# The order of twelve products in an out projection: four float32r products first, or one page at a time

## The chip, the cores and the metric

The kernel runs on one core of one Trainium2 chip. The metric is the device time of one execution in microseconds (us); the time given is the median of several runs.

## The reference

Attention over pooled keys and values, followed by a gated feed-forward layer (SwiGLU) on the 4608 resulting rows:

```python
k_p = k.reshape(B, H, Sp, pool, D).mean(axis=3)          # B=8, H=8, S=576, D=64, pool=8
v_p = v.reshape(B, H, Sp, pool, D).mean(axis=3)
scores = scale * np.matmul(q, k_p.transpose(0, 1, 3, 2))
attn = softmax(scores)
x = np.matmul(attn, v_p) ...                              # as 4608 rows of 512
g = x @ w_gate                                            # 512 x 1536
silu = g * (1.0 / (1.0 + np.exp(-g)))
val = x @ w_val                                           # 512 x 1536
out = silu * val @ w_out                                  # 1536 x 512
```

## The kernel before

The 4608 rows are cut into nine tiles of 512 (`TILE`). The hidden width of 1536 is cut into twelve chunks of 128 (`NCH`), the output width of 512 into four pages of 128 (`NJ`). Everything is computed transposed: the hidden unit or output column lies on the partition, the 512 rows of a tile on the free axis.

To keep float32 precision, each operand of a product is split into a high and a low part. For a tile and a chunk, `side` issues twelve float16 products for the gate and twelve for the value (lines L797 to L799: high by high, high by low, low by high, for each of four slices of x), each into one PSUM bank (`gv`). From these, ScalarE and VectorE make the hidden value h of the chunk, and three copies of it: `hh` (float32r, L1076), `hb` (bfloat16, L1077) and the rest `hl` (bfloat16, L1080).

The out projection of a chunk, `project`, adds the chunk's part to the four pages of the output, which are four PSUM banks `acc`, one for each page j. Each page takes three products of 512 columns: `wo_h` by `hh` in float32r (L824), the weights in bfloat16 by `hl` (L830) and `wo_l` by `hb` (L831), twelve in all. A float32r matmul loads its weights itself (the trace shows it as a load and a matmul of one line); a bfloat16 product has a load instruction of its own ahead of it.

The first tile is written out by hand, with the loading of weights and the first attention pieces between its steps. From the second tile on, `hidden_tiles` runs the loop: for each tile i and chunk c, gate products, value products, the copies of h, and then `flush()`, which issues the projection of the chunk before (its operands have been ready for long; after the last chunk its own projection follows at once). Behind a tile's last projection `store` copies the four pages to SBUF, by VectorE and ScalarE in turn (L838), and issues a DMA for each (L839).

The attention of later tiles runs in the background. At four points of each chunk `slot(vector, scalar)` is called, which issues whichever pieces of it fit: scores (L542, L543), the subtraction of the maximum (L552, L553), values (L658, L659), sums over partitions (L181, L182), and copies, loads and transposes. One of the four points lies inside the projection: it is handed to `project` as `between`, and called after the four float32r products. In the first tile `project` has no `between`.

The order of instructions on each engine is the order in which the program writes them (a manual schedule).

Of the kernel before, what the change touches and what calls it, by code (L numbers as in the profile page):

```python
# [17 lines left out]
P = 128  # L18
# [67 lines left out]
def attention_then_swiglu(  # L86
# [11 lines left out]
    nc = tc.nc  # L98
    B, _, NJ, S = q.shape
# [49 lines left out]
    wo_h = const.tile([P, NCH, DM], F32R, name="wo_h")  # L149
# [668 lines left out]

    def project(acc, c, a, e, hh, hb, hl, begin, end, between=None, wo=wo_b):
        n = e - a  # L820
        for j in range(NJ):
            o = acc[j][:, a:e]
            js = slice(j * P, (j + 1) * P)
            nc.tensor.matmul(o, wo_h[:, c, js], hh[:, :n], start=begin, stop=False)  # L824
        if between:
            between()
        for j in range(NJ):
            o = acc[j][:, a:e]
            js = slice(j * P, (j + 1) * P)
            nc.tensor.matmul(o, wo[:, c, js], hl[:, :n], start=False, stop=False)  # L830
            nc.tensor.matmul(o, wo_l[:, c, js], hb[:, :n], start=False, stop=end)  # L831

    def store(t, acc):
        lo, n, _ = t
        for p in range(NJ // 2):
            ob = mid.tile([P, 2, TILE], F32, name="ob", tag="mid")[:, :, :n]
            for j, copy in ((2 * p, nc.vector.tensor_copy), (2 * p + 1, nc.scalar.copy)):
                copy(out=ob[:, j % 2], in_=acc[j][:, :n])  # L838
                nc.sync.dma_start(out=out[j * P : (j + 1) * P, lo : lo + n], in_=ob[:, j % 2])  # L839
# [67 lines left out]
    def first_tile():  # L907
# [69 lines left out]
        def step_out(k):  # L977
            t = steps[k]
            hb = t["hh"].bitcast(BF16).rearrange("p (n t) -> p n t", t=2)[:, :, 1]
            end = k == len(steps) - 1  # L980
            project(kept["acc"], *t["at"], t["hh"], hb, t["hl"], False, end, wo=wo_up)
# [58 lines left out]
    def hidden_tiles():  # L1040
# [4 lines left out]
        def flush():  # L1045
            if pending:
                acc, last, i, c, *rest = pending.pop()
                wo = wo_b if i > 2 else wo_up
                project(acc(), c, 0, tiles[i][1], *rest, c == 0, last, lambda: slot(*ROOM[2]), wo)
                if last:  # L1050
                    store(tiles[i], acc())
# [92 lines left out]
```

## Time and profile before

| | |
|---|---|
| median of 3 runs | 977.51 us (976.91 to 977.65) |
| profiled execution | 975.54 us, span 973.8 us |
| TensorE matmuls busy | 939.7 us (97%) |
| VectorE, ScalarE, GpSimd busy | 566.0, 461.2, 241.3 us |
| TensorE clock granted | 0.993 of full speed on average |

In a row of the timeline stand the start in us from the span's start, the duration, the engine (PE is TensorE's matmul, PEld its weight load, DVE VectorE, ACT ScalarE, SPq the queue that issues DMAs), the line, the operation, the tiles that it writes and reads, shapes and count, and in brackets the idle time of the engine before it and what ended that. Successive equal instructions are merged into one row. Matmuls are pipelined: the recorded time of one overlaps the next, so the distance from start to start is what one costs. A row of a stretch gives its length, then busy time and count of PE, PEld, DVE, ACT and POOL, the granted clock, the DMA share and GB/s.

### The profile page before, as it was taken

To read this page: it belongs to the slowest core of one execution; us is meant where nothing else is said; L and a number is where in the kernel's file an instruction comes from. 1 tells how busy PE (TensorE), PEld (TensorE's weight loads), DVE (VectorE), ACT (ScalarE), POOL (GpSimd) and SP (SyncE) were. 2 spreads that over 40 slices of the span, in tenths; PEclk is the share of its full clock that TensorE was granted. 3 is DMA by queue.
4 is the path that set the end of the run, shared out by engine and by line. 5 is a ranking of instruction groups with operands and counts; after the bars stand their busy time and mean duration, and the time that the engine had idled before them with its cause. 6 is when DMAs were issued, how large, how long until landed. Compare 5 with 4: busy or idle time off the path is not lost.

```text
span 973.8 us, 14306 instructions
## 1 busy us (share of the span) xinstructions
PE 939.7 (97%) x5486; PEld 498.4 (51%) x5486; DVE 566.0 (58%) x1005; ACT 461.2 (47%) x864; POOL 241.3 (25%) x327
## 2 busy tenths in 40 slices
PE   5779999799999999999999999999999999999998
PEld 4657545354555555554555555554545555444443
DVE  6788877667766675586446675674444454323222
ACT  3898883245554553544254544552454443222222
POOL 4533336035226230521025211620121201000000
PEclk9899999999999999999999999999999999999999
DMA  9855426246437342653047232840231222001001
GB/s 349 237 154 208 154 109 171 80 115 186 92 109 211 102 83 79 187 127 82 13 88 235 57 70 87 251 86 15 77 83 43 71 66 55 11 1 44 0 1 44
DMA packets 155524, 103.02 MB, mean 106 GB/s; under 512 B 113216, under 2 KB 141888, under 8 KB 153920
## 3 DMA queue, kind: packets, MB, share of 16 engines
q1 hardware_dynamic: 155456, 102.11, 37.3%
q8 instruction: 43, 0.70, 0.3%
q14 instruction: 25, 0.20, 0.1%
HBM read 67.63 MB, written 9.44 MB: 79 GB/s over the span
## 4 chain that ended last, share of the span: by engine, by line
PE 87%; DMA 6%; POOL 2%; ACT 2%; issue 1%; DVE 1%; SPq 0%; POOLq 0%; DVEq 0%; ACTq 0%
PE gv L797 18%; PE gv L798 18%; PE gv L799 18%; PE acc L824 10%; PE acc L830 9%; PE acc L831 9%; DMA pt<-half 2%; DMA kr<-k_rows 1%; DMA in<-v_rest 1%; DMA in<-k_rows 1%; PE ps L542 1%; PE ps L658 1%; PE ps L543 1%; PE ps L659 1%; DMA k<-k_rows 1%
## 5 line engine op out<-in xcount | busy, mean ns | idle before, releaser
L797 PE MATMUL gv<-x,wgv_h 128*128 128x512 f16 (+1 forms) x888 | 332.0, 374 | 3.8 <-ACT x L669 1.8
L798 PE MATMUL gv<-x,wgv_h 128*128 128x512 f16 (+1 forms) x888 | 331.8, 374 | 1.3 <-DVE x L673 1.3
L799 PE MATMUL gv<-x,wgv_l 128*128 128x512 f16 (+1 forms) x888 | 331.9, 374 | 0.5 <-DVE wgv_l L253 0.5
L810 DVE SCALAR_TENSOR_TENSOR hf<-hf,gv 128x512 f32<-128x512 f32 (+1 forms) x111 | 74.1, 668 | 171.6 <-ACT hf L807 171.3
L807 ACT ACTIVATE hf<-gv,un 128x512 f32<-128x512 f32 (+1 forms) x111 | 74.8, 674 | 193.9 <-PE gv L799 193.9
L1076 ACT CAST hh<-gv 128x512 fp32r<-128x512 f32 x96 | 56.3, 586 | 227.2 <-DVE gv L815 227.2
L831 PE MATMUL acc<-hb,wo_l 128*128 128x512 bf16 x384 | 145.5, 379 | 0.0
L824 PE MATMUL acc<-hh,wo_h 128*128 128x512 f32 (+1 forms) x444 | 139.5, 436 | 0.0
L799 PEld LDWEIGHTS <-wgv_l 128*128 128x128 f16 x888 | 87.0, 98 | 102.2 <-issue 1.7
L798 PEld LDWEIGHTS <-wgv_h 128*128 128x128 f16 x888 | 87.0, 98 | 98.1 <-issue 4.7
L797 PEld LDWEIGHTS <-wgv_h 128*128 128x128 f16 x888 | 87.4, 98 | 94.3
L1080 DVE TENSOR_TENSOR hl<-gv,hh 128x512 bf16<-128x512 f32 x96 | 66.3, 691 | 111.0 <-ACT hb L1077 111.0
L525 POOL TENSOR_TENSOR box<-qt,box 64x512 f16<-64x512 f32 (+1 forms) x60 | 64.0, 1067 | 227.8 <-issue 160.9
L815 DVE SCALAR_TENSOR_TENSOR gv<-gv,un,hf 128x512 f32<-128x512 f32 (+1 forms) x111 | 82.3, 741 | 63.0 <-PE gv L799 62.3
L830 PE MATMUL acc<-hl,wo_b 128*128 128x512 bf16 x288 | 109.8, 381 | 0.0
L824 PEld LDWEIGHTS acc<-hh,wo_h 128*128 128x128 f32 x444 | 83.2, 191 | 24.2 <-ACT hh L969 0.3
L630 POOL TENSOR_TENSOR half<-sc,half 128x512 f16<-128x512 f32 (+1 forms) x30 | 34.7, 1158 | 215.8 <-ACT half L620 193.6
L831 PEld LDWEIGHTS <-wo_l 128*128 128x128 bf16 x444 | 43.7, 98 | 37.9
L1077 ACT CAST hb<-gv 128x512 bf16<-128x512 f32 x96 | 56.8, 591 | 0.0
L830 PE MATMUL acc<-hl,wo_h 128*128 128x512 bf16 (+1 forms) x156 | 56.7, 368 | 0.0
L830 PEld LDWEIGHTS <-wo_b 128*128 128x128 bf16 x288 | 28.3, 98 | 42.2 <-issue 16.6
L523 ACT ACTIVATE qt<-qt,inv 128x512 f32<-128x512 f32 (+1 forms) x60 | 40.9, 682 | 0.0
(143 smaller groups left out, 1121.5 us busy)
## 6 DMA issues: line engine op xcount, KB each, us to landing
ws<-w_all SPq DMA_DIRECT2D x12, 1536.0 KB, 7.1
qt<-q_twice SPq DMA_DIRECT2D x48, 256.0 KB, 3.2
out_t<-ob SPq DMA_DIRECT2D x36, 256.0 KB, 2.3
in<-k_rows SPq DMA_DIRECT2D x12, 576.0 KB, 3.9
in<-q_rows SPq DMA_DIRECT2D x12, 576.0 KB, 5.2
in<-v_main SPq DMA_DIRECT2D x12, 512.0 KB, 4.3
in<-v_rest SPq DMA_DIRECT2D x12, 512.0 KB, 5.7
qt<-q_rows SPq DMA_DIRECT2D x8, 256.0 KB, 4.3
```

The lines of the kernel that those rows point to most:

```text
L525: nc.gpsimd.tensor_sub(o[rows], qt[rows], o[rows])
L797: nc.tensor.matmul(o, wh, x["h"][:, j, a:e], start=(j == 0), stop=False)
L798: nc.tensor.matmul(o, wh, x["l"][:, j, a:e], start=False, stop=False)
L799: nc.tensor.matmul(o, wl, x["h"][:, j, a:e], start=False, stop=(j == NJ - 1))
L807: nc.scalar.activation(hf, gate, AF.Tanh, scale=un[:, c, 0:1])
L810: nc.vector.scalar_tensor_tensor(out=hf, in0=hf, scalar=1.0, in1=gate, op0=ALU.add, op1=ALU.mult)
L815: nc.vector.scalar_tensor_tensor(out=out, in0=val, scalar=un[:, c, 2:3], in1=hf, op0=ALU.mult, op1=ALU.mult)
L824: nc.tensor.matmul(o, wo_h[:, c, js], hh[:, :n], start=begin, stop=False)
L830: nc.tensor.matmul(o, wo[:, c, js], hl[:, :n], start=False, stop=False)
L831: nc.tensor.matmul(o, wo_l[:, c, js], hb[:, :n], start=False, stop=end)
L1077: nc.scalar.copy(hb[:, :n], val)
L1080: nc.vector.tensor_sub(hl[:, :n], val, hh[:, :n].bitcast(F32))
```

## The change

Where `project` is given a `between`, that is in the 96 projections of the second to ninth tile, the twelve products are issued page by page: one float32r product, then the two bfloat16 ones of the same page. The slot's background work is called after two pages. Without `between`, in the first tile, the order stays as it was.

```diff
     def project(acc, c, a, e, hh, hb, hl, begin, end, between=None, wo=wo_b):
         n = e - a
-        for j in range(NJ):
-            o = acc[j][:, a:e]
+
+        def high(j):
             js = slice(j * P, (j + 1) * P)
-            nc.tensor.matmul(o, wo_h[:, c, js], hh[:, :n], start=begin, stop=False)
-        if between:
-            between()
-        for j in range(NJ):
-            o = acc[j][:, a:e]
-            js = slice(j * P, (j + 1) * P)
+            nc.tensor.matmul(acc[j][:, a:e], wo_h[:, c, js], hh[:, :n], start=begin, stop=False)
+
+        def low(j):
+            o, js = acc[j][:, a:e], slice(j * P, (j + 1) * P)
             nc.tensor.matmul(o, wo[:, c, js], hl[:, :n], start=False, stop=False)
             nc.tensor.matmul(o, wo_l[:, c, js], hb[:, :n], start=False, stop=end)
+
+        if between:
+            for j in range(NJ):
+                if j == NJ // 2:
+                    between()
+                high(j)
+                low(j)
+            return
+        for j in range(NJ):
+            high(j)
+        for j in range(NJ):
+            low(j)
```

On TensorE, the last projection of the program stood like this before (`acc_8681` to `acc_8684` are the four pages; the rest repeats for the other pages):

```order
L824 MATMUL acc_8681<-hh,wo_h 128x512
L824 MATMUL acc_8682<-hh,wo_h 128x512
L824 MATMUL acc_8683<-hh,wo_h 128x512
L824 MATMUL acc_8684<-hh,wo_h 128x512
L830 LDWEIGHTS wo_b
L830 MATMUL acc_8681<-hl,wo_b 128x512
L831 LDWEIGHTS wo_l
L831 MATMUL acc_8681<-hb,wo_l 128x512
```

and with the change, where the two bfloat16 lines are L828 and L829, its first two pages are:

```order
L824 MATMUL acc_8681<-hh,wo_h 128x512
L828 LDWEIGHTS wo_b
L828 MATMUL acc_8681<-hl,wo_b 128x512
L829 LDWEIGHTS wo_l
L829 MATMUL acc_8681<-hb,wo_l 128x512
L824 MATMUL acc_8682<-hh,wo_h 128x512
L828 LDWEIGHTS wo_b
L828 MATMUL acc_8682<-hl,wo_b 128x512
L829 LDWEIGHTS wo_l
L829 MATMUL acc_8682<-hb,wo_l 128x512
```

Each float32r product now has bfloat16 products on both sides, and each page's last product comes three after that of the page before, where it came two after.

In 20 of the 96 projections the slot inside issues small matmuls. On TensorE, at the end of the values of one such projection (`pt` the attention weights, `box` the values, `acc_5005` to `acc_5008` the pages), before:

```order
L659 LDWEIGHTS pt
L659 MATMUL ps<-box,pt 128x64
L830 LDWEIGHTS wo_b
L830 MATMUL acc_5005<-hl,wo_b 128x512
L831 LDWEIGHTS wo_l
L831 MATMUL acc_5005<-hb,wo_l 128x512
```

and with the change:

```order
L659 LDWEIGHTS pt
L659 MATMUL ps<-box,pt 128x64
L824 MATMUL acc_5007<-hh,wo_h 128x512
L828 LDWEIGHTS wo_b
L828 MATMUL acc_5007<-hl,wo_b 128x512
L829 LDWEIGHTS wo_l
L829 MATMUL acc_5007<-hb,wo_l 128x512
```

The small matmuls are now followed by the float32r product of the third page; ahead of them stand six products of the projection, where four stood. On the other engines and in the DMA queue the order is unchanged.

## The prediction

> **What bounds the kernel now.** I read the page's totals first, then the chain that ended last, then the busy time of a late stretch, and only then single rows on TensorE.
>
> ```profile
> span 973.8 us, 14306 instructions
> PE 939.7 (97%) x5486; PEld 498.4 (51%) x5486; DVE 566.0 (58%) x1005; ACT 461.2 (47%) x864; POOL 241.3 (25%) x327
> PE 87%; DMA 6%; POOL 2%; ACT 2%; issue 1%; DVE 1%; SPq 0%; POOLq 0%; DVEq 0%; ACTq 0%
> ...
> 510.00:810.00 300.00, 300.00 (x1759) 152.70 (x1758) 170.08 (x308) 138.26 (x279) 70.48 (x94) 1.00 0.35 95
> ...
> PE ps L658 <- issue: 1.0, 1, 1.0
> PE ps L658 <- DVE sc L553: 0.5, 1, 0.5
> ```
>
> The fourth line is a stretch of the trace, from 510 to 810 us: TensorE is busy for all of its 300 us, the other engines for less than 60% of it, and the granted clock is 1.00. The last two lines are all waits of TensorE that the list of waits has from 190 us to the end: 1.5 us. So in the part that the change touches (from the second tile on), the time is the sum of the distances between matmul starts, and any nanosecond added to a distance is added to the run. Work taken off another engine would buy nothing.
>
> So I need those distances. A matmul's recorded duration (0.38 us) overlaps the next one; only starts count. Here is one out projection, before, with the loads of its weights (PEld); the rows for the second, third and fourth float32r product come from narrow cuts of the same timeline, where they are not merged.
>
> ```profile
> 606.66 0.38 PE L799 MATMUL gv<-x,wgv_l 128*128 128x512 f16 x1
> 606.66 0.87 PEld L824 LDWEIGHTS acc<-hh,wo_h 128*128 128x128 f32 x4
> 607.11 0.39 PE L824 MATMUL acc<-hh,wo_h 128*128 128x512 f32 x1
> 607.34 0.39 PE L824 MATMUL acc<-hh,wo_h 128*128 128x512 f32 x1
> 607.57 0.40 PE L824 MATMUL acc<-hh,wo_h 128*128 128x512 f32 x1
> 607.80 0.10 PEld L830 LDWEIGHTS <-wo_b 128*128 128x128 bf16 x1 [0.27 <-issue]
> 607.81 0.39 PE L830 MATMUL acc<-hl,wo_b 128*128 128x512 bf16 x1
> 608.03 0.38 PE L831 MATMUL acc<-hb,wo_l 128*128 128x512 bf16 x1
> 608.03 0.10 PEld L830 LDWEIGHTS <-wo_b 128*128 128x128 bf16 x1
> ...
> 955.85 0.38 PE L799 MATMUL gv<-x,wgv_l 128*128 128x512 f16 x1
> 957.23 0.38 PE L831 MATMUL acc<-hb,wo_l 128*128 128x512 bf16 x1
> 963.70 0.38 PE L799 MATMUL gv<-x,wgv_l 128*128 128x512 f16 x1
> ```
>
> From 957.23 to 963.70 stand 30 distances between 16-bit products: 6.47 / 30 = 0.2157 us each. From the last 16-bit product ahead of the float32r ones (L799) to the second bfloat16 product behind them (L831) are 6 distances: 1.37 us in the first case, 1.38 in the second, 1.375 as their mean, where six plain ones take 1.294. So a group of four float32r products costs T = 0.081 us more than its length. Where does it sit? Between one float32r product and the next lie 0.46 / 2 = 0.23 us; with the rounding of the rows between 0.2275 and 0.2325. I take 0.231, so each of the three inner distances is r = 0.0155 too long (0.012 to 0.017 by the rounding), 0.046 together. The other 0.035 lie at entry and exit. The exit is plain in the loads: a bfloat16 load normally starts with the product ahead of it (608.03 beside 608.03), but the first one behind a float32r product starts at 607.80, after 0.27 us without a load, just ahead of its own matmul. It is not loaded early.
>
> **The change part by part.** No product, load, copy or transfer is added or removed, and VectorE, ScalarE, GpSimd and the DMA queue keep their orders instruction by instruction. Only TensorE's order changes, in 96 out projections (8 tiles by 12 chunks).
>
> First, the grouping. Before, a projection has one entry and one exit, after, four. Alone, a float32r product costs entry plus exit, T - 3r = 0.081 - 0.046 = 0.035 us. Four cost 0.140, against T = 0.081 for the group: +0.059 in round numbers, and from 3T - 12r with r = 0.0155, 0.243 - 0.186 = +0.057 us. 96 x 0.057 = **+5.5 us**. With r at its rounding bounds it is 0.101 and 0.041 per projection, 9.7 and 3.9 us. The entry is now from a bfloat16 product and not a float16 one; the very last projection of the run shows this case:
>
> ```profile
> 966.37 0.38 PE L831 MATMUL acc<-hb,wo_l 128*128 128x512 bf16 x1
> 966.40 1.28 PE L824 MATMUL acc<-hh,wo_h 128*128 128x512 f32 x4
> 967.52 0.39 PE L830 MATMUL acc<-hl,wo_b 128*128 128x512 bf16 x1
> 967.75 0.38 PE L831 MATMUL acc<-hb,wo_l 128*128 128x512 bf16 x1
> ```
>
> 966.37 to 967.75 is 1.38 us, the same as from float16. A lone float32r product is nowhere in this trace; that its entry and exit cost what a group's do is the step I lean on.
>
> Second, the background work. In 20 projections the slot in the middle issues small matmuls (15 times the values L658 and L659, 4 times these and sums, once sums alone). Before, a bfloat16 product follows them; after, the third page's float32r one.
>
> ```profile
> 616.62 0.19 PE L659 MATMUL ps<-box,pt 128*128 128x64 f16 x1
> 616.65 0.38 PE L830 MATMUL acc<-hl,wo_b 128*128 128x512 bf16 x1
> ...
> 108.84 0.19 PE L649 MATMUL ps<-pt,vst_f 96*128 96x64 f16 x1
> 108.87 1.18 PE L824 MATMUL acc<-hh,wo_h 128*128 128x512 f32 x4
> 110.12 0.39 PE L831 MATMUL acc<-hh,wo_l 128*128 128x512 bf16 x1
> ```
>
> A bfloat16 product comes 0.03 us after a small one (616.62, 616.65), so nothing is exposed. The nearest case of a float32r product behind a small one is in the first tile: from L649 to the second bfloat16 product are 1.28 us. Behind a 512-column product it was 1.375; the small one should save 0.216 - 0.03 = 0.186 but saves 0.095, so 0.09 us of the float32 load stand open. 20 x 0.09 = **+1.8 us**; at least 0, if other loads are ahead, at most 20 x 0.19 = 3.8, if a whole load (0.87 us for four overlapping ones, so about 0.19 from one to its end) shows. I take the row, which is the same pair of kinds.
>
> Third, the slot's work is reached later: two pages (six products) stand ahead of it and not four products. That is two distances more, 0.43 us. Two projections wait there now, for VectorE to be done with the buffer:
>
> ```profile
> 229.65 1.29 PE L824 MATMUL acc<-hh,wo_h 128*128 128x512 f32 x4
> 231.35 0.46 DVE L553 TENSOR_TENSOR sc<-ps,mx 128x288 f32<-128x288 f32 x1
> 231.91 0.19 PE L658 MATMUL ps<-box,pt 128*128 128x64 f16 x1 [0.98 <-issue]
> ...
> 415.22 1.28 PE L824 MATMUL acc<-hh,wo_h 128*128 128x512 f32 x4
> 417.04 0.19 PE L658 MATMUL ps<-box,pt 128*128 128x64 f16 x1 [0.55 <-DVE sc L553]
> ...
> 615.06 1.28 PE L824 MATMUL acc<-hh,wo_h 128*128 128x512 f32 x4
> 616.18 0.20 PE L658 MATMUL ps<-box,pt 128*128 128x64 f16 x1
> ```
>
> Undisturbed, L658 comes 1.12 us after the group's first record (615.06, 616.18); here 2.26 and 1.82, so 1.14 and 0.70 us are waited. VectorE's time is set by its own queue, so bfloat16 products that now run in the wait take 0.43 us off each: **-0.9 us** (0 if VectorE shifts along, -1.85 if both waits go). The values come 0.43 us later for those behind them, VectorE and ScalarE, which idle 40% and more; I cost that at nothing, and its cover is the rest of the projection and the next 24 products.
>
> Fourth, the end. The pages' last products are now three apart and not two, so copies and stores start earlier, the last one's copy excepted.
>
> ```profile
> 969.46 0.59 ACT L838 COPY ob<-acc 128x512 f32<-128x512 f32 x1 [0.28 <-PE acc L831]
> 969.78 0.40 SPq L839 DMA_DIRECT2D out_t<-ob  x1
> 970.27 0.41 SPq L839 DMA_DIRECT2D out_t<-ob  x1
> ```
>
> The last copy ends at 970.05 but its store is issued at 970.27, behind the third one (to 970.18). With the third one a product (0.22 us) earlier, the last goes out at about 970.1: **-0.2 us**, between 0 and -0.25. Its cover for a loss is the last hl: the first bfloat16 product now needs it at 966.9 or so, and in the trace of before it is written by 966.8. Buffers hh and hb are held up to 1.3 us longer, with a whole chunk of 7.85 us until they are written again: nothing.
>
> Sum: 5.5 + 1.8 - 0.9 - 0.2 = +6.2 us. The profiled execution took 975.54 us (973.8 of span); the sum makes 981.7 of it. It ran 2 us under the median, 977.51, so for the median I predict **983.7 us**, +0.6%.
>
> **The rivals.** (a) Order is free: entry and exit are hidden when a float32r product stands alone, so that twelve products take the same time in any order. Then the first two terms are 0 and only the waits and the end remain: 977.5 - 1.1 = 976.4. For it: the matmuls and their weights are the same. Against it: the 0.27 us gap of loads in each group. The Trainium skill ("TensorE: Matmul & The Clock Gate", Step-by-step: what each phase is for) states this rule: the queue pulls weight loads ahead, and the next weights load while the present matmul runs. By it the change would come out at 976.4. The trace agrees between 16-bit products, and ahead of a float32r one (the load at 606.66), but not behind one (607.80). Chance 0.07.
>
> (b) Faster: the open load at the exit is what a run of four float32r products leaves behind, because each takes longer than its distance; a lone one leaves nothing. Each would then cost only its entry, T - 3r less the exit. The exit is 607.57 to 608.03, 0.46 against 0.431, so 0.029 of the 0.035; 0.006 x 4 = 0.024 remain against 0.081. 96 x (0.024 - 0.081) = -5.5; with +1.8 - 1.1, -4.8: 972.7. It decides if a lone product costs under about 0.018 us in all (0.081 / 4, less 0.7 us spread over 384 products). For it: no row shows a lone one. Against it: the distances inside the group are even, with nothing that grows. Chance 0.05.
>
> (c) Dearer: the first float32r product's true start does not show (its record spans the wait). From L799 to the second one are 0.45 us, 0.018 more than two distances. If this all is entry, and the first inner distance is plain, a lone product costs T - 2r = 0.050, a projection 0.200 - 0.081 = +0.119, 96 of them 11.4 us: +12.1, 989.6. For it: a float32 load takes about 0.19 of 0.216 us, little room. Against it: the other inner distances are long too. Chance 0.08.
>
> **How the numbers follow.** The forecast itself has 0.80. With half the way to each bound, all on one side, it reaches from 4.7 + 0.9 - 1.4 - 0.2 = +4.0 to 7.6 + 2.8 - 0.45 - 0.1 = +9.9, 981.5 to 987.4; with the scatter of the runs shown, 0.7 us, 980.8 to 988.1. That leaves out (a), (b) and (c), 0.20, and is my range. What a measurement can tell here is about 0.2%, 2 us: faster is (b), 0.05; the same is (a), 0.07; slower are the forecast and (c), 0.88.
>
> **What would show it.** A chunk late in the run, 955.85 to 963.70 or 7.85 us now, should take 7.90 to 7.91. The loads of bfloat16 weights behind a float32r product should each show the gap of about 0.27 us, four to a projection. The two waits at L658 should be about 0.4 us shorter. The forecast is wrong if a lone product's entry and exit, from the product ahead to the second behind, do not take about 0.68 us (three distances and 0.035), or if new waits on TensorE appear.

## The result, and the profile after

The changed kernel takes 982.39 us (median of six runs, 979.93 to 983.71), the kernel before 977.21 (six runs, 975.99 to 979.72). The ratio is 1.0056 with a 95% interval of 1.0041 to 1.0071: slower by 5.5 us by the ratio, by 5.2 between the medians. The forecast was 983.7.

The page after, with the lines that answer to those of before:

```profile
span 981.9 us, 14306 instructions
PE 948.8 (97%) x5486; PEld 478.3 (49%) x5486; DVE 566.8 (58%) x1005; ACT 461.5 (47%) x864; POOL 242.2 (25%) x327
PE 87%; DMA 7%; DVE 2%; POOL 2%; issue 1%; ACT 0%; SPq 0%; POOLq 0%; DVEq 0%; ACTq 0%
```

The counts are the same, TensorE is still the bound, and its busy time has grown with the span. The span of this profile is 8.1 us longer than before, more than the times say, so first look where the stretches differ. These are the starts of the first projection that the change touches, in the timelines of TensorE before, after, and in a second profile of the unaltered changed kernel (run "again"):

```profile
188.36 0.58 PE L824 MATMUL acc<-hh,wo_h 128*128 128x512 f32 x1
...
191.79 0.58 PE L824 MATMUL acc<-hh,wo_h 128*128 128x512 f32 x1
...
189.54 0.58 PE L824 MATMUL acc<-hh,wo_h 128*128 128x512 f32 x1
```

The first tile, in which no instruction differs, took 188.4, 191.8 and 189.5 us: it scatters. Behind it lie 973.8 - 188.4 = 785.4 us before, 981.9 - 191.8 = 790.1 after, and 980.2 - 189.5 = 790.7 in the second profile. So the change costs 4.7 to 5.3 us, and I compare the part behind the first tile, projection by projection, from here on.

A late projection and the two ends of 14 late chunks, after:

```profile
861.91 0.38 PE L799 MATMUL gv<-x,wgv_l 128*128 128x512 f16 x1
...
972.42 0.38 PE L799 MATMUL gv<-x,wgv_l 128*128 128x512 f16 x1
972.42 0.19 PEld L824 LDWEIGHTS acc<-hh,wo_h 128*128 128x128 f32 x1
972.45 0.58 PE L824 MATMUL acc<-hh,wo_h 128*128 128x512 f32 x1
972.87 0.10 PEld L828 LDWEIGHTS <-wo_b 128*128 128x128 bf16 x1 [0.26 <-issue]
972.87 0.39 PE L828 MATMUL acc<-hl,wo_b 128*128 128x512 bf16 x1
973.10 0.38 PE L829 MATMUL acc<-hb,wo_l 128*128 128x512 bf16 x1
973.10 0.19 PEld L824 LDWEIGHTS acc<-hh,wo_h 128*128 128x128 f32 x1
973.13 0.58 PE L824 MATMUL acc<-hh,wo_h 128*128 128x512 f32 x1
```

A chunk takes 110.51 / 14 = 7.893 us, where it took 7.850. From the product ahead of a lone float32r one (972.42) to the second behind it (973.10) are 0.68 us, the length forecast for entry and exit. The load of the float32r weights starts early (972.42), that of the bfloat16 weights behind it does not (972.87, after 0.26 us without a load). The page's groups have the sum of these gaps, before (first line) and after:

```profile
L830 PEld LDWEIGHTS <-wo_b 128*128 128x128 bf16 x288 | 28.3, 98 | 42.2 <-issue 16.6
...
L828 PEld LDWEIGHTS <-wo_b 128*128 128x128 bf16 x288 | 27.6, 96 | 72.5 <-issue 72.2
```

The last number of a line counts the long gaps alone. Of the same 288 loads at most one in four stands behind a float32r product before, and now all do: 72.2 / 288 = 0.25 us each in the mean. Most of each gap is covered by the product that runs: a chunk has three more such gaps and grew by only 0.043 us. That the uncovered rest of the gaps is the whole cost is the reading that fits; the runs show what a way in and out costs together, not its split between the two.

### The profile page after: what moved, and what is told of

Read it like the earlier page. It is cut to its first block, busy times and chain, and to the rows that moved or that the text cites. A ratio compares the mean times of both kernels' runs of the same rounds, so it can differ in the third digit from the quotient of the medians.

```text
span 981.9 us, 14306 instructions
## 1 busy us (share of the span) xinstructions
PE 948.8 (97%) x5486; PEld 478.3 (49%) x5486; DVE 566.8 (58%) x1005; ACT 461.5 (47%) x864; POOL 242.2 (25%) x327
## 4 chain that ended last, share of the span: by engine, by line
PE 87%; DMA 7%; DVE 2%; POOL 2%; issue 1%; ACT 0%; SPq 0%; POOLq 0%; DVEq 0%; ACTq 0%
PE gv L797 18%; PE gv L798 18%; PE gv L799 18%; PE acc L824 10%; PE acc L828 10%; PE acc L829 9%; DMA kr<-k_rows 1%; DMA in<-v_rest 1%; DMA in<-k_rows 1%; DMA pt<-half 1%; PE ps L542 1%; PE ps L658 1%; DMA ws<-w_all 1%; PE ps L543 1%; PE ps L659 1%
## 5 line engine op out<-in xcount | busy, mean ns | idle before, releaser
L824 PE MATMUL acc<-hh,wo_h 128*128 128x512 f32 (+1 forms) x444 | 237.7, 552 | 0.2 <-ACT hh L979 0.2
L829 PE MATMUL acc<-hb,wo_l 128*128 128x512 bf16 x384 | 145.5, 379 | 0.0
L828 PE MATMUL acc<-hl,wo_b 128*128 128x512 bf16 x288 | 112.3, 390 | 0.0
L828 PEld LDWEIGHTS <-wo_b 128*128 128x128 bf16 x288 | 27.6, 96 | 72.5 <-issue 72.2
L828 PE MATMUL acc<-hl,wo_h 128*128 128x512 bf16 (+1 forms) x156 | 57.5, 373 | 0.2 <-DVE hl L983 0.2
L829 PEld LDWEIGHTS <-wo_l 128*128 128x128 bf16 x444 | 44.4, 100 | 4.1 <-POOL un L995 0.2
```

The source lines that it names most:

```text
L824: nc.tensor.matmul(acc[j][:, a:e], wo_h[:, c, js], hh[:, :n], start=begin, stop=False)
```

## The experiments

The theory: each run of float32r products between 16-bit ones costs an entry and an exit, whatever its length, and the rest of the loss is a float32 load left open behind small matmuls. The rival in the first runs: the new order writes one PSUM bank three times in a row, and this costs. The edits are shown against the changed kernel, that of "two" against the kernel before; three dots stand for lines left out. "bf_page", "bf_group" and "again" ran once each, so I use their traces and not their times.

**Two pages at a time** (run "pairs").

```diff
-            for j in range(NJ):
-                if j == NJ // 2:
+            for j in range(0, NJ, 2):
+                if j:
                     between()
                 high(j)
+                high(j + 1)
                 low(j)
+                low(j + 1)
```

> Two pages at a time: two float32r products, then their four bfloat16 ones, the slot's work between the two halves. Theory (each run of float32r products pays one entry and one exit, about 0.032 us in all, and 0.0155 for each further product of the run): a projection costs 2 x (0.032 + 0.0155) = 0.095 over its length, against 0.081 in a group of four and 0.126 page by page; a late chunk takes 7.86 us, and the whole is about 2 us slower than the kernel before (96 x 0.014 + 20 x 0.09 for the slot's small matmuls - 1 for waits and end). Rival (the cost comes from three products in a row into one PSUM bank): here no float32r product is followed by one of its own bank, so a late chunk takes 7.85 us or less, and the whole is as before or up to 1 us faster.

The ratio to before was 1.0031 (1.0013 to 1.0049), 785.4 became 789.0 us behind the first tile. Rows of the timeline, 13 chunks apart and one half of a projection:

```profile
849.69 0.38 PE L799 MATMUL gv<-x,wgv_l 128*128 128x512 f16 x1
...
951.99 0.38 PE L799 MATMUL gv<-x,wgv_l 128*128 128x512 f16 x1
952.01 0.81 PE L824 MATMUL acc<-hh,wo_h 128*128 128x512 f32 x2
952.67 0.39 PE L828 MATMUL acc<-hl,wo_b 128*128 128x512 bf16 x1
952.90 0.38 PE L829 MATMUL acc<-hb,wo_l 128*128 128x512 bf16 x1
```

102.30 / 13 = 7.869 us a chunk, between the 7.850 of one run of four and the 7.893 of four lone ones. The theory's 7.86 is nearly met, the bank's 7.85 is missed: here no float32r product is followed by one of its own bank, and yet two exits cost more than one. Behind the first tile the whole grew by 3.6 us and not by 2; TensorE's two waits for VectorE were longer here than before, 1.2 and 0.9 us (more on them under run "mid").

**No float32r product at all** (runs "bf_page" and "bf_group"): in `project`, when `between` is given,

```diff
+            if between:
+                nc.tensor.matmul(acc[j][:, a:e], wo[:, c, js], hb[:, :n], start=begin, stop=False)
+                return
             nc.tensor.matmul(acc[j][:, a:e], wo_h[:, c, js], hh[:, :n], start=begin, stop=False)
```

"bf_group" has the grouped order besides:

```diff
             for j in range(NJ):
-                if j == NJ // 2:
-                    between()
                 high(j)
+            between()
+            for j in range(NJ):
                 low(j)
```

> The changed kernel's order, but from the second tile on the float32r product of each page is replaced by a bfloat16 one of the same size (bfloat16 weights by hb; the output has the precision of bfloat16 there). The same banks are written in the same order. Theory (the cost is the way into and out of a float32r product): a late chunk takes 36 plain distances of 0.2158, 7.77 us. Rival (three products in a row into one bank cost 0.043 us a projection): 7.81 us, 0.04 more than the grouped twin.

> The grouped order of the kernel before, with the same replacement of float32r products by bfloat16 ones from the second tile on. Both theories: a late chunk takes 7.77 us, 0.08 less than with four float32r products in a group.

The first product of a projection, 15 chunks apart, in the page order's timeline; and the group of four in the grouped order's chain, 17 chunks apart:

```profile
839.70 0.38 PE L825 MATMUL acc<-hb,wo_b 128*128 128x512 bf16 x1
956.25 0.38 PE L825 MATMUL acc<-hb,wo_b 128*128 128x512 bf16 x1
...
826.00 0.86 PE acc L825 x4
958.09 0.86 PE acc L825 x4
```

116.55 / 15 = 7.770 and 132.09 / 17 = 7.770 us. With bfloat16 alone the order of pages is free to the nanosecond: the rival of the banks falls. (Behind the first tile "bf_page" took 777.0 us and "bf_group" 778.9; the two waits, 1.2 us together against 2.7, and the end make this difference.) And 7.770 is the floor, 36 plain distances. Over it, a projection with runs of one costs 7.893 - 7.770 = 0.123, or 0.031 a run; with runs of two 0.099, 0.050 a run; with one run of four 0.080. So the second product of a run adds 0.019 us, the third and the fourth 0.015 each; as one line, a run of n costs about 0.031 + 0.0165 (n - 1) us.

**The slot's work, not ahead of a float32r product** (run "slot"): page by page, but `between` is called inside `low` of the second page, ahead of its last product.

```diff
-        def low(j):
+        def low(j, middle=None):
...
             nc.tensor.matmul(o, wo[:, c, js], hl[:, :n], start=False, stop=False)
+            if middle:
+                middle()
             nc.tensor.matmul(o, wo_l[:, c, js], hb[:, :n], start=False, stop=end)
...
-                if j == NJ // 2:
-                    between()
                 high(j)
-                low(j)
+                low(j, between if j == NJ // 2 - 1 else None)
```

> Page by page as in the changed kernel, but the slot's work is issued ahead of the last bfloat16 product of the second page, so that no float32r product follows small matmuls directly. Theory (the 0.09 us in 20 projections are the float32 load that stands open behind a small matmul): those projections cost the same 0.04 to 0.05 us over the kernel before as the other 76, the whole is about 1.8 us faster than the changed kernel and 3 us slower than the kernel before. Rival (the interruption of the projection itself costs it): those projections keep their 0.13 to 0.15, and the whole stays at +4.7.

Here are the ends of the values in the changed kernel, and in this one:

```profile
320.88 0.19 PE L659 MATMUL ps<-box,pt 128*128 128x64 f16 x1
320.88 0.19 PEld L824 LDWEIGHTS acc<-hh,wo_h 128*128 128x128 f32 x1
320.91 0.47 PE L824 MATMUL acc<-hh,wo_h 128*128 128x512 f32 x1
321.23 0.39 PE L828 MATMUL acc<-hl,wo_h 128*128 128x512 bf16 x1
...
268.55 0.19 PE L659 MATMUL ps<-box,pt 128*128 128x64 f16 x1
268.58 0.38 PE L831 MATMUL acc<-hb,wo_l 128*128 128x512 bf16 x1
268.61 0.58 PE L824 MATMUL acc<-hh,wo_h 128*128 128x512 f32 x1
269.03 0.39 PE L828 MATMUL acc<-hl,wo_h 128*128 128x512 bf16 x1
```

In the changed kernel the float32 load can start only at 320.88, with the last small matmul, and the float32r product has its bfloat16 successor at 321.23, 0.35 us on; one distance of 0.216 and the small product's 0.03 would be 0.25. In "slot" the load lies under a full product. The 18 such projections without a wait took 0.139 us more than before in the mean in the changed kernel, and 0.052 (0.037 to 0.065) in "slot", close to the 0.044 of the 76 others. The term is shown. The whole did not gain as much: 789.5 us behind the first tile, because the waits for VectorE were longer (next run), and a ratio of 1.0024 (1.0007 to 1.0040).

**Grouped as before, the slot's work later** (run "mid").

```diff
             for j in range(NJ):
+                high(j)
+            for j in range(NJ):
                 if j == NJ // 2:
                     between()
-                high(j)
                 low(j)
```

> The grouped order of the kernel before, but the slot's work comes after the bfloat16 products of two pages, 0.86 us later than before. Theory: one entry and one exit as before, so a late chunk takes 7.85 us; only the waits for VectorE change, at most -1.8 us and, if VectorE's work shifts along in one of the two, about -0.9. The whole is 0 to 1 us faster than before, less than can be told by time. Rival (small matmuls between bfloat16 products cost as they do ahead of a float32r one): 20 x 0.09, about 1 us slower.

The chunk stays at 7.850 us, and the list of TensorE's waits behind 190 us is, in the changed kernel (two lines), in its second profile (two), in "slot" (two) and here (one):

```profile
PE ps L658 <- DVE sc L553: 0.6, 1, 0.6
PE ps L658 <- issue: 0.2, 1, 0.2
...
PE ps L658 <- issue: 0.8, 1, 0.8
PE ps L658 <- DVE sc L553: 0.6, 1, 0.6
...
PE ps L658 <- DVE sc L553: 1.1, 1, 1.1
PE ps L658 <- issue: 0.9, 1, 0.9
...
PE ps L658 <- issue: 0.4, 1, 0.4
```

Before, it was 1.0 and 0.5. Reaching the values 0.86 us later takes 1.1 us off the two waits; reaching them 0.43 later, as the change does, takes off 0.7 in one profile and next to nothing in the other, and in "pairs", which reaches them as late, the waits grew by 0.6. What moves them stands on VectorE ahead of the subtraction (L553) that the values wait for; at the first wait before, in the changed kernel and in its second profile:

```profile
228.56 2.33 DVE L267 TENSOR_REDUCE box<-in 128x144 f32<-128x1152 f32 x1 [0.52 <-DMA in<-k_rows]
...
231.88 2.25 DVE L267 TENSOR_REDUCE box<-in 128x144 f32<-128x1152 f32 x1 [0.77 <-DMA in<-k_rows]
...
230.21 2.27 DVE L267 TENSOR_REDUCE box<-in 128x144 f32<-128x1152 f32 x1 [1.38 <-DMA in<-k_rows]
```

VectorE idles until a transfer of `k_rows` has landed, sums keys (L267), and starts the subtraction 2.7 to 2.8 us after that sum's start. The sum starts 1.09, 1.36 and 0.77 us ahead of the projection's first float32r product (229.65, 233.24 and 230.98), and the waits are 1.0, 0.2 and 0.8. The same chain stands at both waits in all traces but that of "two", which I did not read for it. So the waits follow a landing that moved by 0.6 us between two profiles of one program; why it moves stays open.

The part behind the first tile took 784.2 us, 1.2 less than before; by time it is no difference, 0.9991 (0.9975 to 1.0006).

**Two chunks' projections at once** (run "two"): the opposite of the change, eight float32r products and then sixteen bfloat16 ones, every second chunk.

```diff
-            if pending:
-                acc, last, i, c, *rest = pending.pop()
-                wo = wo_b if i > 2 else wo_up
-                project(acc(), c, 0, tiles[i][1], *rest, c == 0, last, lambda: slot(*ROOM[2]), wo)
...
+            if len(pending) == 2 or (whole and pending):
...
+                project_all(some, 0, tiles[i][1], lambda: slot(*ROOM[2]))
...
+            elif pending:
+                slot(*ROOM[2])
```

> The opposite direction: two chunks' projections are issued together, eight float32r products and then sixteen bfloat16 ones, every second chunk (three buffers for each of hh, hb and hl). Theory: 48 of 96 entries and exits of 0.032 us go, so two late chunks take 15.67 us and not 15.70, and the whole is about 1.5 us faster than before. Rival (order is free or the cost is one of each product): 15.70 us and no change; rival (a longer run of float32r products costs more at its exit): 15.70 or more, and slower.

It was slower, 1.0238 (1.0215 to 1.0260), and none of the expectations named why. Rows of one late pair of chunks, and the largest of TensorE's waits behind 190 us:

```profile
951.55 0.38 PE L834 MATMUL acc<-hb,wo_l 128*128 128x512 bf16 x1
959.10 0.69 DVE L1088 TENSOR_TENSOR hl<-gv,hh 128x512 bf16<-128x512 f32 x1 [1.19 <-ACT hb L1085]
959.32 0.38 PE L799 MATMUL gv<-x,wgv_l 128*128 128x512 f16 x1
959.84 0.38 PE L797 MATMUL gv<-x,wgv_h 128*128 128x512 f16 x1
962.21 0.38 PE L799 MATMUL gv<-x,wgv_l 128*128 128x512 f16 x1
962.24 2.21 PE L827 MATMUL acc<-hh,wo_h 128*128 128x512 f32 x8
964.52 0.38 PE L834 MATMUL acc<-hb,wo_l 128*128 128x512 bf16 x1
967.55 0.38 PE L834 MATMUL acc<-hb,wo_l 128*128 128x512 bf16 x1
...
PE ps L542 <- DVE box L759: 8.9, 5, 1.8
```

In a chunk without a projection the value products (959.84) come 0.52 us after the last gate product (959.32), 0.3 too late: their bank is read until 959.79 by the copy of hl (959.10 + 0.69) of the chunk before. The projection that used to stand between covered that copy. With such waits the pair takes 16.00 us and not 15.70. They are the smaller part of the loss, some 4 to 5 us over the run: the listed waits behind 190 us sum to 20.7 us, where they were 1.5, and 8.9 of them are scores that wait for VectorE. I did not follow those back. My own price was wrong too: joining two runs saves an entry and exit but adds one inner distance, 0.031 - 0.0165 = 0.015 and not 0.032. The run of eight costs some 0.15 us, as the formula says (0.147): from 962.21 to 964.52 are ten distances in 2.31 us, where ten plain ones take 2.16.

**The end, and a version faster than both** (runs "again" and "both"). "again" is the changed kernel unaltered. "both" is "mid", with only the very last projection page by page:

```diff
+            if paged:
+                for j in range(NJ):
+                    high(j)
+                    low(j)
+                return
+            for j in range(NJ):
+                high(j)
             for j in range(NJ):
                 if j == NJ // 2:
                     between()
-                high(j)
                 low(j)
...
-                project(acc(), c, 0, tiles[i][1], *rest, c == 0, last, lambda: slot(*ROOM[2]), wo)
+                project(acc(), c, 0, tiles[i][1], *rest, c == 0, last, lambda: slot(*ROOM[2]), wo, last and i == len(tiles) - 1)
```

> The changed kernel once more, unaltered. From the first projection of the second tile to the end its profile took 790.1 us, the kernel before 785.4; ahead of it 191.8 and 188.4 us, though no instruction differs there. Theory (the stretch ahead scatters from run to run, the rest does not): 789.5 to 790.7 behind, anything from 188 to 192 ahead. Rival (the change lengthens the first tile): 191.5 or more ahead.

> Grouped as before with the slot's work after two pages of bfloat16 products (which took 1.2 us off the part behind the first tile), and only the very last projection page by page, so that the last stores are spread. Theory (the changed kernel's end was 0.62 us shorter, in spite of 0.04 for the order, because stores start earlier and land sooner): from the start of the last projection to the end 6.75 us and not 7.37, 783.6 us behind the first tile in all, about 0.2% faster than before, at the edge of what time can tell. Rival (the shorter end was chance of one profile): 7.3 us at the end, 784.2 in all.

"again" has 189.5 us ahead and 790.7 behind: the longer first tile was scatter. From the start of the last projection to the end it was 7.37 us before and in "mid", and 6.75 after, in "again" and in "both". The rows after, and the median of the last four stores from issue to landing, before and after:

```profile
975.16 0.58 PE L824 MATMUL acc<-hh,wo_h 128*128 128x512 f32 x1
978.26 0.59 ACT L848 COPY ob<-acc 128x512 f32<-128x512 f32 x1 [0.77 <-PE acc L829]
978.87 0.33 SPq L849 DMA_DIRECT2D out_t<-ob  x1
...
out_t<-ob SPq DMA_DIRECT2D x4, 256.0 KB, 2.3
...
out_t<-ob SPq DMA_DIRECT2D x4, 256.0 KB, 2.0
```

The last store is issued 0.02 us after its copy ends (978.85), where it was 0.22 (970.05, 970.27): that is the 0.2 forecast. The rest is the last store itself, which took 2.07 us from issue to landing, where it took 2.53. Before, the four were issued 0.43 to 0.49 us apart and landed 0.61 to 0.70 apart, each taking longer than the one before; after, they are issued 0.56 to 0.79 apart. "both" took 783.8 us behind the first tile, and its ratio to before is 0.9976 (0.9961 to 0.9990), 2.4 us faster; the traces account for 1.6.

## Why the prediction was right, point by point

The mechanism held: TensorE was the bound, the lone float32r product's exit stands open as in the group, and the two large terms are where the sum put them. The sizes, term by term:

- **Grouping, forecast +5.5.** The 76 projections without small matmuls took 0.044 us more each in the mean, so 96 give +4.2; a late chunk came to 7.893 us, just under the 7.90 that I had as the least. The inner distance was read rightly: in the trace of before, the two that show are 0.2311 and 0.2317 us in the mean of 96 projections, 0.0156 over a plain one in the mean. What was off is the step that I leaned on, that a lone product costs what a group's entry and exit do: it costs 0.031 and not 0.035, because a run's second product, whose distance from the first no row shows, adds 0.019 and not 0.0155. That r was so close was luck in part. Two ends rounded to 0.01 us leave the distance between 0.225 and 0.235, twice the width that I gave, and the term anywhere from about 1 to 13 us.
- **Small matmuls, forecast +1.8.** 0.139 - 0.044 = 0.095 us in each, 20 x 0.095 = +1.9. The row from the first tile was the right neighbour, and "slot" shows the cause.
- **Waits, forecast -0.9.** -0.7 in one profile of the changed kernel, -0.1 in the other. The step "VectorE's time is set by its own queue" fails: ahead of both waits VectorE waits for a transfer of `k_rows`. At the second one the sum behind it starts 1.01 us ahead of the projection, where it was 1.53, and the wait grew by 0.1; at the first one the wait differs by 0.6 between two profiles of one program. What I had as a term is mostly scatter, and the -0.7 near the forecast is luck.
- **End, forecast -0.2.** -0.66 against the order's own 0.04. I costed the queue's issue, which measured as said, and left out that spread stores land sooner.

4.2 + 1.9 - 0.7 - 0.66 = +4.7 and, with the second profile's waits, +5.3: the 4.7 and 5.3 of the two traces. The errors of the first and the last terms were in the same direction, and the forecast of +6.2 was high by about one microsecond.

Rival (a), that order is free, falls for float32r and holds for bfloat16 alone ("bf_page", "bf_group"). By the Trainium skill ("TensorE: Matmul & The Clock Gate", Step-by-step: what each phase is for) the next weights load while a matmul runs; the trace agrees for loads ahead of a float32r product and not for the bfloat16 load behind one, ahead of which stood 0.25 us without a load in the mean of 288. Rival (b), a lone product without exit, would have made the chunk shorter than 7.850; it is 7.893. Rival (c), 0.050 for a lone product, is refuted by 0.031.

Why the bfloat16 load is not started under a float32r product was not settled. The runs show that it is so, and that another float32r product behind it costs about half as much (0.015 to 0.019 against 0.031).

## What to carry to other kernels

Where the matmul engine is the bound, count transitions between kinds of products, not only products: here a lone float32r product between 16-bit ones cost 0.031 us and a further one behind it about half of that, so grouping them is worth keeping, and small matmuls are best followed by a product whose weights load fast. Before joining more, see what the products between cover: taking one projection out of every second chunk opened a wait twenty times the saving. And a cost that no row shows, here a lone product's, is not yet known from the rows around it: 0.004 us each made 1.3 us of the forecast. Rows rounded to 0.01 us cannot settle it; a distance over many chunks can.

## What the runs showed that I had not expected

- The first tile, untouched, took between 188.4 and 191.8 us in the profiles of before, after, "again", "pairs", "slot", "mid" and "both". Comparing spans alone would have given 8.1 us for a change of 4.7.
- Four stores of 256 KB landed in 2.0 us in the median when issued over 1.9 us, and in 2.3 when issued over 1.4; the end of the run gained more from this than from the earlier issue.
- Three products in a row into one bank cost nothing: 7.770 us a chunk in either order.
